# First keys ahead of the last seeds' stores, first maxima by pairs, and copies that lie interleaved, in a kernel of a state-space convolution beside attention

## The chip, the cores and the metric

The kernel runs on one core of one Trainium2 chip. The metric is the time of one execution on the device in microseconds (us); the time of a version is the median of its runs.

## The reference

Two independent operators on sequences of 2048 rows and 448 columns, float32, whose results are put side by side:

```python
def _A_ref(u, log_A_real, A_imag, C_real, C_imag, log_dt, D_skip):
    dt = jnp.exp(log_dt)
    A = -jnp.exp(log_A_real) + 1j * A_imag
    C = (C_real + 1j * C_imag) * dt[:, None]
    P = jnp.exp((A * dt[:, None])[:, :, None] * pos[None, None, :])
    K = 2.0 * jnp.einsum("dn,dnl->dl", C, P).real      # 448 x 2048, from 256 states each
    ...                                                # y = causal convolution of u with K, by FFT
    return y + u * D_skip[None, None, :]

def _B_ref(x, wqkv, wo):                               # 16 heads of 28
    q, k, v = qkv[0], qkv[1], qkv[2]
    scores = jnp.einsum("bhqd,bhkd->bhqk", q, k) * scale
    p = _softmax(scores, axis=-1)
    o = jnp.einsum("bhqk,bhkd->bhqd", p, v)
    return (lambda x, *d: x.transpose(*d))(o, 0, 2, 1, 3).reshape(B, S, D) @ wo

    return jnp.concatenate([a, b], axis=-1)
```

## The kernel before, in words

Everything is written with a tile framework that works out the waits between instructions. All of it lies in one function, `body`; a helper object records every instruction, which is why every row of the profile names line 75 and groups are told apart by the names of their tiles.

**First part.** Its instructions are put in order on each engine by the framework's planner, which goes by the order of the program and its own idea of when operands are ready. Two kinds of work are woven together over 41 stages (`n_stage`, the loop `for t in range(n_stage)`).

- Projections. The input `x` is taken in four chunks of 512 rows (`load_x`, tiles `xn`, transposed into `xh` and `xl`). Forty-eight jobs, twelve a chunk, make keys, queries (`qk_proj`, 12 matmuls each, for one group of four heads) and values (`v_proj`). Every float32 value is held as a high and a low part. `project()` issues the matmuls of the next job and then the evacuation (`evac`) of the one before: ScalarE writes the high part, VectorE the low part, both into a tile `hl` of which there are three, and SyncE stores it to DRAM (`k<-hl`, `q<-hl`). The weights lie in the memory that later holds the keys of the first group (`k0_t`, by the name `khat`), head index for head index, so the keys of head j can only be loaded when the projections of group j are over.
- Seeds. For eight groups `o` of channels, `seeds(o)` lists thirteen steps that make starting values for the powers of the state-space kernel. A group starts four stages after the one before. Two tiles come out: `se` in a buffer of the ring `qhat` (three buffers, shared with the query tiles) and `sg` (two buffers). `put_g` and `put_e`, the last two steps, store them (`sd<-sg`, `sd<-qhat`).

The list `ahead` puts loads for the attention into the stages: key differences (`load_kd`, from stage `A0` on), the first query tile (`load_q(0)`, in two halves at stages `A1` and `A1 + 1`), the keys of heads 0 to 2 (`load_k`, at the stages in `KW`). After the last projection come the keys of head 3, the second query tile, and the values. All of these DMAs are issued by SyncE, in order of the program.

A query or key tile holds, for 28 features and two spare rows of a head, four copies of 32 rows on the 128 partitions: high and low parts combined so that one matmul gives all four products. A copy lies on 32 neighbouring partitions, and each copy is a DMA of its own.

**First maxima.** The softmax subtracts the row maximum. For query block 0, sixteen tiles of 128 queries go against 2048 keys in four steps (`max_mm(0, i, kc)`). Steps 0 and 1 belong together: step 0 multiplies with the difference of two key blocks (`kdif`), ScalarE takes the relu into `rl`, and step 1 multiplies with the second block and lets VectorE add `rl` and reduce in one pass; relu(a - b) + b is the larger of a and b. Steps 2 and 3 are plain reductions (`mx`). Each step takes one of five PSUM tiles (`pt` or `pm`). `max_join` takes the maximum of the three columns, `max_end` transposes it on TensorE and makes a negative high and low part (`mh`), and `max_put` writes these by two DMAs into the spare rows of the query tile (`qhat<-mh`), so that the score matmul subtracts the maximum by itself.

**Second part.** From here on the program's own order is kept on every engine (`KEPT["a"]`). Three seed tiles are loaded (`load_sd`, `sdb<-sd`), the first three tiles of the next query block's maxima (`LEAD`) are made, and then 256 slots follow with score matmuls (`pss`), exponentials (`p`), products with the values (`po`), maxima of the next query block, and the convolution's work in between, by `ORDER` and due times counted in slots. Keys, queries and key differences of later groups are loaded by the same helpers.

Of the kernel before, what the change touches and what calls it, by code (L numbers as in the profile page):

```python
# [18 lines left out]
D = 448  # L19

H = 16
DH = 28
G = 4
HG = H // G
CQ = 512
# [15 lines left out]
PS = 1  # L41
SGB, XB, XL = 2, 5, 4
K0, KP, KD, UP = 0, 3.5, 4, 3
A0, A1, KW = 26, 34, (33, 35, 36)

N1 = 32
N2 = 64
# [43 lines left out]
def body(ctx, tc, a, out):  # L91
# [53 lines left out]
    def load_k(g, j, p):  # L145
        if j == 0:
            t = k0_t if g == 0 else p.tile([128, HG, L], F32R, name="khat")
            kt_g[g] = [t[:, i] for i in range(HG)]
        for r in range(4):
            nc.sync.dma_start(kt_g[g][j][32 * r:32 * r + 32, :].bitcast(F32), k_d[g][r % 2, 32 * j:32 * j + 32, :])  # L150

    v_g = {}

    def load_v(g, c):
        v_g[g, c] = t = v_p.tile([128, NK // NQ, HG, 32], F32, name="v", bufs=5)
        nc.sync.dma_start(t.rearrange("p t h e -> p t (h e)"), v_d[c][:, g])

    def load_kd(g, j, rows=range(4)):
        if 0 in rows:
            kd_g[g, j] = kd_p.tile([128, CQ], F32R, name=f"kdif{j}")  # L160
        t = kd_g[g, j]
        for r in rows:
            nc.sync.dma_start(t[32 * r:32 * r + 32].bitcast(F32), kd_d[g][r % 2, 32 * j:32 * j + 32, :])

    def load_q(u, rows=range(4)):
        g, c = divmod(u, NQ)
        if 0 in rows:
            q_u[u] = q_p.tile([128, HG, CQ], F32R, name="qhat", bufs=3)
        t = q_u[u]
        for r in rows:  # L170
            nc.sync.dma_start(t[32 * r:32 * r + 32].bitcast(F32), q_d[g][c][r // 2].rearrange("(j p) q -> p j q", j=HG))

    def max_mm(u, i, kc, ps=w_tile):

# [16 lines left out]
            nc.tensor.matmul(pm, q, kt[:, kc * CQ:(kc + 1) * CQ], start=True, stop=True)  # L191
            nc.vector.tensor_reduce(mx, pm, axis=AX.X, op=ALU.max)

    def max_join(u):
        m_u[u, 1] = q_p.tile([128, HG * 4], F32, name="m1", bufs=2)
        nc.vector.tensor_reduce(m_u[u, 1], m_u[u].rearrange("p a b c -> p (a b) c"), axis=AX.X, op=ALU.max)

    def max_end(u, ps):
        nc.tensor.transpose(ps[:16, :128], m_u[u, 1], ident)
# [3 lines left out]
                                       op0=ALU.mult, op1=ALU.subtract)  # L203
        mh_u[u] = mh

    def max_put(u):
        for i in range(2):
            nc.sync.dma_start(q_u[u][DH + i:DH + i + 1, :, :].rearrange("p h (t q) -> p (h t) q", t=4).bitcast(F32),
                                mh_u[u][:, i, :].bitcast(F32))


    with ExitStack() as st:
# [12 lines left out]
        def load_x(c):  # L225
            xs = x[c * CQ:(c + 1) * CQ, :].rearrange("(t p) d -> p t d", p=128)
            for h in range(2):
                xns[c, h] = y_p.tile([128, 2, D], F32, name="xn", bufs=3)
                nc.sync.dma_start(xns[c, h], xs[:, 2 * h:2 * h + 2, :])

        load_x(0)
# [24 lines left out]
                                                            ap=[[256, JF // 4], [JF * 256, 4], [1, 256]]))  # L256

        dt_all = s_p.tile([PO, 5, NO], F32, name="dt_all")
        ldt = s_p.tile([NO, PO], F32, name="ldt")
        t = a["A_log_dt"]  # L260
        for f in range(2):
            nc.sync.dma_start(ldt[4 * f:4 * f + 4, :].rearrange("o (j i) -> o j i", j=4), bass.AP(
# [16 lines left out]

        def exact_exp(y, x_, shape):  # L280

            t = lambda n, d=F32: s_p.tile(shape, d, name=n)
            ts, stt = nc.vector.tensor_scalar, nc.vector.scalar_tensor_tensor
            x1, kf, r1, p, ki = t("x1"), t("kf"), t("r1"), t("px"), t("ki", I32)
            ts(x1, x_, -87.0, 88.0, op0=ALU.max, op1=ALU.min)
            ts(kf, x1, 1.4426950408889634, MAGIC, op0=ALU.mult, op1=ALU.add)
            ts(kf, kf, MAGIC, None, op0=ALU.subtract)
            stt(r1, kf, -0.693359375, x1, op0=ALU.mult, op1=ALU.add)
            stt(r1, kf, 2.12194440e-4, r1, op0=ALU.mult, op1=ALU.add)
            ts(p, r1, 1.0 / 5040, 1.0 / 720, op0=ALU.mult, op1=ALU.add)  # L290
            for q in (120.0, 24.0, 6.0, 2.0, 1.0):
                nc.vector.tensor_tensor(p, p, r1, ALU.mult)
                ts(p, p, 1.0 / q, None, op0=ALU.add)
            nc.vector.tensor_tensor(p, p, r1, ALU.mult)
            ts(kf, kf, 127.0, 8388608.0, op0=ALU.add, op1=ALU.mult)
            nc.vector.tensor_copy(ki, kf)
            stt(y, p, 1.0, ki.bitcast(F32), op0=ALU.add, op1=ALU.mult)

        dt8 = s_p.tile([NO, PO], F32, name="dt8")
        exact_exp(dt8, ldt, [NO, PO])  # L300
        dt_o = s_p.tile([NO, PO], F32, name="dt_o")
        nc.vector.tensor_copy(dt_o.rearrange("o (i j) -> o j i", j=4), dt8.rearrange("o (j i) -> o j i", j=4))

        def turn_dt():
# [153 lines left out]
        def qk_proj(c, s, g):  # L458
            pp = w_tile()
            n = 0  # L460
            for k in range(NCK):
                for i, x_ in ((0, xh), (1, xh), (0, xl)):
                    nc.tensor.matmul(pp, w_g[:, i, s, k, g].rearrange("p h e -> p (h e)"), x_[k],
                                     start=n == 0, stop=n == 3 * NCK - 1)
                    n += 1

            def evac():
                hl = x_p.tile([128, 2, CQ], F32R, name="hl", bufs=3)
                th, tl = hl[:, 0], hl[:, 1]
                if s == 1:  # L470
                    nc.scalar.activation(th, pp, AF.Identity, bias=kones)
                    nc.vector.scalar_tensor_tensor(tl, pp, kones, th.bitcast(F32), op0=ALU.add, op1=ALU.subtract)
                else:
                    nc.scalar.activation(th, pp, AF.Copy)
                    nc.vector.tensor_tensor(tl, pp, th.bitcast(F32), ALU.subtract)
                if s == 1 and c < 2:
                    HC = CQ // 2
                    kb = y_p.tile([128, HC], F32, name="kb")
                    dhl = y_p.tile([128, 2, HC], F32R, name="dhl")
                    dh, dl = dhl[:, 0], dhl[:, 1]  # L480
                    nc.scalar.activation(kb, pp[:, HC:], AF.Copy)
# [32 lines left out]
        stages = [seeds(o) for o in range(NO)]  # L514
        n_stage = SP * (NO - 1) + len(stages[0])
        slots = [[] for _ in range(n_stage)]
        for o in range(NO):
            for i, st_ in enumerate(stages[o]):
                slots[max(SP * o + (i or -2), 0)] += st_
# [6 lines left out]
        for i in range(2):  # L526
            ahead[A1 + i].append(lambda i=i: load_q(0, range(2 * i, 2 * i + 2)))

        for j, t in enumerate(KW):
            ahead[t].append(lambda j=j: load_k(0, j, k0_p))  # L530

        def project():

            e = work.pop(0)() if work else None
            while pend:
                pend.pop(0)()
            if e:
                pend.append(e)

        for t in range(n_stage):  # L540
            while work and n_work - len(work) < n_work * (t + 1) / PW:
                project()
            for f in slots[t] + ahead.get(t, []):
                f()
            if t + 1 == PW:
                project()
                wst.close()
                load_k(0, HG - 1, k0_p)
                load_q(1)
                for c in range(NQ):  # L550
                    load_v(0, c)
        xst.close()
        more = [lambda: ps_t.tile([128, CQ], F32, name="pt")] * 2 + [w_tile] * 3
        for i in range(16):
            for kc in range(4):
                max_mm(0, i, kc, more[(4 * i + kc) % 5])
        nc.scalar.activation(half_pi[:1], half_pi[:1], AF.Exp)
        max_join(0)
        max_end(0, ps_t.tile([128, CQ], F32, name="pt"))
        max_put(0)  # L560
        sst.close()


# [59 lines left out]

    sds, egs = {}, {}

    def load_sd(b):
        sds[b] = g_p.tile([128, SDF], F32, name="sdb", bufs=4)
        nc.sync.dma_start(sds[b], sd_d[b // BO][b % BO])

    def k_seeds(b):  # L630

# [241 lines left out]

    nc.kept = KEPT["a"]
    for b in range(3):
        load_sd(b)
    for i in range(LEAD):
        for kc in range(4):
            max_mm(1, i, kc)
# [260 lines left out]
```

## Time and profile before

| | us |
|---|---|
| median of 3 runs | 1284.48 (1284.33 to 1285.08) |
| profiled execution | 1284.77 |
| its span on the core | 1283.0 |
| TensorE busy in the span | 1221.8 |
| last projection matmul starts | 183.22 |
| first matmul of the first maxima starts | 194.86 |
| first score matmul (`pss`) starts | 234.70 |

Times inside the span count from its start. PE is TensorE, PEld its weight loads, DVE VectorE, ACT ScalarE, POOL GpSimd, SP SyncE (SPq its queue, in which each DMA is an issue). A row of the order of time gives the start, the time it took, engine, operation and tiles, and in brackets the idle time of the engine before it with what ended that. A row of the waits gives the total, the count and the longest. A row of a stretch gives its length, then for each engine busy time and instructions, then the clock granted to TensorE as a share, the busy share of the 16 DMA engines, and GB/s. A wait for several semaphores is put down to the one that came last by the profile.

### The profile page before, as it was taken

The numbers are of one execution on the slowest core, as the hardware profiler recorded it, in microseconds if no ns is written. First come the engines' busy times: TensorE is split into PE (matmuls) and PEld (weight loads), VectorE is DVE, ScalarE is ACT, GpSimd is POOL, SyncE is SP. The second block draws the span as 40 slices with busy tenths as digits, with TensorE's granted clock in tenths as the row PEclk, the third lists the DMA queues.
The fourth block names the chain that finished last, engine by engine and source line by source line (L and its number), as shares of the span: only waits on it lengthen the run. The fifth ranks groups of instructions, "written<-read, shape, count | busy, mean of one in ns | idle before, by whom it ended". The sixth has DMA issues, their size and how long they took to land.

```text
span 1283.0 us, 33256 instructions
## 1 busy us (share of the span) xinstructions
PE 1221.8 (95%) x12625; PEld 696.6 (54%) x12625; DVE 931.8 (73%) x2106; ACT 957.1 (75%) x2142; POOL 844.4 (66%) x728
## 2 busy tenths in 40 slices
PE   7988857999999999999999999999999999999997
PEld 5867743555555555555555555555555555544433
DVE  5788878877877787878778988888897645645111
ACT  4979852688888888888888888888887756656552
POOL 2466750698878888887689999989995222324321
PEclk9989888899999999999999999999999999999999
DMA  7867799447764645478643233742325543657666
GB/s 212 264 243 264 247 307 273 127 95 171 182 153 103 153 133 147 133 204 206 169 101 90 63 73 81 163 103 71 82 60 148 166 143 134 204 162 238 200 162 173
DMA packets 200088, 205.36 MB, mean 160 GB/s; under 512 B 95992, under 2 KB 158520, under 8 KB 197880
## 3 DMA queue, kind: packets, MB, share of 16 engines
q1 hardware_dynamic: 199928, 203.23, 57.1%
q8 instruction: 100, 1.64, 0.6%
q14 instruction: 60, 0.49, 0.1%
HBM read 120.73 MB, written 82.18 MB: 158 GB/s over the span
## 4 chain that ended last, share of the span: by engine, by line
PE 75%; DVE 11%; ACT 4%; POOL 4%; issue 3%; DMA 2%; SPq 0%; POOLq 0%; ACTq 0%; DVEq 0%
PE pm L75 42%; PE pss L75 16%; PE po L75 16%; DVE mx L75 2%; POOL e L75 1%; ACT tri L75 1%; DVE sg L75 1%; DVE tri L75 1%; DVE rl L75 1%; DVE px L75 1%; DVE hl L75 1%; DMA khat<-k 1%; DVE qhat L75 1%; POOL p L75 1%; DMA tri<-in_B_wqkv 1%
## 5 line engine op out<-in xcount | busy, mean ns | idle before, releaser
L75 ACT ACTIVATE p<-pss 128x512 f32<-128x512 f32 x1024 | 561.4, 611 | 112.2 <-PE pss L75 106.8
L75 PE MATMUL pss<-qhat,khat 128*128 128x512 f32 x1024 | 403.4, 400 | 1.7 <-ACT p L75 1.7
L75 DVE TENSOR_REDUCE mx<-pm 128x1 f32<-128x512 f32 x500 | 321.7, 684 | 110.2 <-PE pm L75 108.0
L75 PE MATMUL pm<-khat,qhat 128*128 128x512 f32 x749 | 327.2, 440 | 3.2 <-DVE mx L75 2.1
L75 POOL TENSOR_TENSOR e<-e,sdb 128x256 f32<-128x256 f32 x168 | 201.8, 1201 | 118.2 <-ACT e L75 108.9
L75 PE MATMUL po<-p,v 128*32 128x512 f32 x2048 | 269.2, 594 | 0.0
L75 POOL TENSOR_TENSOR e<-e,eu 128x256 f32<-128x256 f32 x168 | 248.2, 1477 | 13.2
L75 PEld LDWEIGHTS pm<-khat,qhat 128*128 128x128 f32 x749 | 141.9, 190 | 199.1 <-ACT p L75 49.5
L75 DVE CUSTOM_DVE_ANT_0 rl<-pm,rl 128x512 f32<-128x512 f32 x249 | 171.5, 689 | 65.5 <-ACT rl L75 62.4
L75 PEld LDWEIGHTS pss<-qhat,khat 128*128 128x128 f32 x1024 | 190.7, 189 | 46.5 <-issue 10.8
L75 POOL TENSOR_TENSOR eu<-e,sdb 128x256 f32<-128x256 f32 x168 | 201.9, 1202 | 0.0
L75 POOL TENSOR_TENSOR p<-pr,pr 64x448 f32<-64x448 f32 x64 | 73.1, 1142 | 159.6 <-PE pm L75 134.2
L75 ACT ACTIVATE rl<-pm 128x512 f32<-128x512 f32 x249 | 151.2, 607 | 20.9 <-PE pm L75 16.4
L75 DVE TENSOR_TENSOR g<-g,zg 128x128 f32<-128x128 f32 x392 | 162.2, 414 | 3.4
L75 PE MATMUL pm<-kdif,qhat 128*128 128x512 f32 x249 | 101.3, 407 | 2.4 <-DVE mx L75 1.3
L75 PE MATMUL pm<-xh,khat 112*128 112x512 f32 x256 | 86.9, 421 | 13.7 <-DVE hl L75 5.2
L75 DVE TENSOR_TENSOR zg<-g,zg 128x128 f32<-128x128 f32 x224 | 87.9, 393 | 5.0
L75 PEld LDWEIGHTS pm<-e,g 128*32 128x32 f32 x3584 | 57.2, 109 | 43.8 <-issue 16.7
L75 DVE TENSOR_TENSOR pr<-pm,ub 128x448 f32<-128x448 f32 x64 | 37.0, 620 | 56.4 <-PE pm L75 42.0
L75 PE MATMUL pm<-e,g 128*32 128x64 f32 x3584 | 73.0, 222 | 1.9 <-POOL e L75 1.9
L75 ACT ACTIVATE y<-pm 128x448 f32<-128x448 f32 x48 | 26.5, 553 | 58.2 <-PE pm L75 34.1
L75 ACT ACTIVATE ub<-pm 128x224 f32<-128x224 f32 (+1 forms) x96 | 38.8, 449 | 39.7 <-PE pm L75 37.4
(134 smaller groups left out, 1445.3 us busy)
## 6 DMA issues: line engine op xcount, KB each, us to landing
sdb<-sd SPq DMA_DIRECT2D x56, 336.0 KB
khat<-k SPq DMA_DIRECT2D x64, 256.0 KB
qhat<-q SPq DMA_DIRECT2D x64, 256.0 KB
sd<-sg SPq DMA_DIRECT2D x8, 1456.0 KB
k<-hl SPq DMA_DIRECT2D x16, 512.0 KB
q<-hl SPq DMA_DIRECT2D x16, 512.0 KB
mw<-in_mw SPq DMA_DIRECT2D x16, 512.0 KB
sd<-qhat SPq DMA_DIRECT2D x8, 896.0 KB
```

What stands on the lines that cost most here:

```text
L75: i = f(*args, **kw)
```

## The change

- The four copies of keys, key differences and queries lie interleaved: copy r takes every fourth partition from r on (`[r::4]`) instead of 32 neighbours. The row of maxima goes to the partitions that follow from it.
- The first query tile is loaded from stage 31 on instead of 34. The keys of the first three heads are loaded by `project()` itself, each behind the evacuation that follows the end of its weights; those of head 3 ahead of the last evacuation.
- The two stores of seed group 6 (`kept_e`, `kept_g`) leave their stages: one goes between the first values and the second query tile, the other behind all values.
- The query evacuations of the last chunk use the three input tiles `xn` (widened from 448 to 512 columns) instead of `hl`.
- Steps 2 and 3 of the first maxima are done as a pair as well (`max_pair`): step 2 accumulates two matmuls, with the query tile and its negative `q_neg`, into the difference, relu on ScalarE, and step 3 adds and reduces. `q_neg` is made by four ScalarE copies. `max_join` then reads two columns.
- The two row DMAs of the first maxima and the load of the first seed tile are issued by ScalarE instead of SyncE.
- The small temporaries of the channel time steps lie in a seed buffer.

```diff
-A0, A1, KW = 26, 34, (33, 35, 36)
+A0, A1 = 26, 31
...
-            nc.sync.dma_start(kt_g[g][j][32 * r:32 * r + 32, :].bitcast(F32), k_d[g][r % 2, 32 * j:32 * j + 32, :])
+            nc.sync.dma_start(kt_g[g][j][r::4, :].bitcast(F32), k_d[g][r % 2, 32 * j:32 * j + 32, :])
...
-            nc.sync.dma_start(t[32 * r:32 * r + 32].bitcast(F32), kd_d[g][r % 2, 32 * j:32 * j + 32, :])
+            nc.sync.dma_start(t[r::4].bitcast(F32), kd_d[g][r % 2, 32 * j:32 * j + 32, :])
...
-            nc.sync.dma_start(t[32 * r:32 * r + 32].bitcast(F32), q_d[g][c][r // 2].rearrange("(j p) q -> p j q", j=HG))
+            nc.sync.dma_start(t[r::4].bitcast(F32), q_d[g][c][r // 2].rearrange("(j p) q -> p j q", j=HG))
+
+    def max_pair(i, kc, ps, q_neg):
+        j, t = divmod(i, 4)
+        ts = slice(t * 128, (t + 1) * 128)
+        pm, kt = ps(), kt_g[0][j]
+        if kc == 2:
+            nc.tensor.matmul(pm, q_u[0][:, j, ts], kt[:, 2 * CQ:3 * CQ], start=True, stop=False)
+            nc.tensor.matmul(pm, q_neg[:, j, ts], kt[:, 3 * CQ:], start=False, stop=True)
+            rl_u[0, i] = kd_p.tile([128, CQ], F32, name="rl", bufs=2)
+            nc.scalar.activation(rl_u[0, i], pm, AF.Relu)
+        else:
+            nc.tensor.matmul(pm, q_u[0][:, j, ts], kt[:, 3 * CQ:], start=True, stop=True)
+            rl = rl_u.pop((0, i))
+            nc.vector.tensor_tensor_reduce(rl, pm, rl, 1.0, -3.0e38, ALU.add, ALU.max, m_u[0][:, j, t, 1:2])
...
-    def max_put(u):
+    def max_put(u, queue=nc.sync):
         for i in range(2):
-            nc.sync.dma_start(q_u[u][DH + i:DH + i + 1, :, :].rearrange("p h (t q) -> p (h t) q", t=4).bitcast(F32),
+            queue.dma_start(q_u[u][4 * (DH + i):4 * (DH + i) + 1, :, :].rearrange("p h (t q) -> p (h t) q", t=4).bitcast(F32),
                                 mh_u[u][:, i, :].bitcast(F32))
...
-                xns[c, h] = y_p.tile([128, 2, D], F32, name="xn", bufs=3)
+                xns[c, h] = y_p.tile([128, 2, CQ], F32, name="xn", bufs=3)[:, :, :D]
...
-                hl = x_p.tile([128, 2, CQ], F32R, name="hl", bufs=3)
+                if c == NQ - 1 and s == 0:
+                    hl = y_p.tile([128, 2, CQ], F32, name="xn", bufs=3).bitcast(F32R)
+                else:
+                    hl = x_p.tile([128, 2, CQ], F32R, name="hl", bufs=3)
...
+        kept_g, kept_e = (stages[NO - 2][i] for i in (-2, -1))
+        stages[NO - 2][-2:] = []
...
-        for j, t in enumerate(KW):
-            ahead[t].append(lambda j=j: load_k(0, j, k0_p))
-
         def project():
 
-            e = work.pop(0)() if work else None
+            j, last = divmod(len(work) - 1, 2)
+            e = work.pop(0)() if work else load_k(0, HG - 1, k0_p)
             while pend:
                 pend.pop(0)()
             if e:
                 pend.append(e)
+            if e and not last and j < HG - 1:
+                load_k(0, HG - 2 - j, k0_p)
...
                 wst.close()
-                load_k(0, HG - 1, k0_p)
+                load_v(0, 0)
+                kept_e.pop()()
                 load_q(1)
-                for c in range(NQ):
+                for c in range(1, NQ):
                     load_v(0, c)
+                kept_g.pop()()
         xst.close()
         more = [lambda: ps_t.tile([128, CQ], F32, name="pt")] * 2 + [w_tile] * 3
+        n_st = ExitStack()
+        q_neg = pool(n_st, "n_p").tile([128, HG, CQ], F32R, name="q_neg")
+        for j in range(HG):
+            nc.scalar.activation(q_neg[:, j], q_u[0][:, j].bitcast(F32), AF.Copy, scale=-1.0)
         for i in range(16):
             for kc in range(4):
-                max_mm(0, i, kc, more[(4 * i + kc) % 5])
+                f, kw = (max_mm, (0, i, kc)) if kc < 2 else (max_pair, (i, kc))
+                f(*kw, more[(4 * i + kc) % 5], *([q_neg] if kc > 1 else []))
         nc.scalar.activation(half_pi[:1], half_pi[:1], AF.Exp)
-        max_join(0)
+        n_st.close()
+        max_join(0, 2)
         max_end(0, ps_t.tile([128, CQ], F32, name="pt"))
-        max_put(0)
+        max_put(0, nc.scalar)
...
-    def load_sd(b):
+    def load_sd(b, queue=nc.sync):
         sds[b] = g_p.tile([128, SDF], F32, name="sdb", bufs=4)
-        nc.sync.dma_start(sds[b], sd_d[b // BO][b % BO])
+        queue.dma_start(sds[b], sd_d[b // BO][b % BO])
...
     for b in range(3):
-        load_sd(b)
+        load_sd(b, nc.sync if b else nc.scalar)
```

More of the change, by code (lines that the diff above doesn't have):

```diff
@@ L192, in max_mm, with max_join @@
             nc.vector.tensor_reduce(mx, pm, axis=AX.X, op=ALU.max)
-    def max_join(u):
+    def max_join(u, n=3):
         m_u[u, 1] = q_p.tile([128, HG * 4], F32, name="m1", bufs=2)
-        nc.vector.tensor_reduce(m_u[u, 1], m_u[u].rearrange("p a b c -> p (a b) c"), axis=AX.X, op=ALU.max)
+        nc.vector.tensor_reduce(m_u[u, 1], m_u[u].rearrange("p a b c -> p (a b) c")[:, :, :n], axis=AX.X, op=ALU.max)
     def max_end(u, ps):
@@ L258, in body @@
         dt_all = s_p.tile([PO, 5, NO], F32, name="dt_all")
-        ldt = s_p.tile([NO, PO], F32, name="ldt")
+        small = s_p.tile([128, BO, SDF - F_G], F32, name="sg", bufs=SGB)
+        small = iter([small[:NO, i, :PO] for i in range(BO)] + [small[:NO, i, PO:2 * PO] for i in range(BO)])
+        ldt = next(small)
         t = a["A_log_dt"]
@@ L280, in exact_exp @@
         def exact_exp(y, x_, shape):
-            t = lambda n, d=F32: s_p.tile(shape, d, name=n)
+            t = lambda n, d=F32: next(small) if d == F32 else next(small).bitcast(d)
             ts, stt = nc.vector.tensor_scalar, nc.vector.scalar_tensor_tensor
@@ L297, in exact_exp @@
             stt(y, p, 1.0, ki.bitcast(F32), op0=ALU.add, op1=ALU.mult)
-        dt8 = s_p.tile([NO, PO], F32, name="dt8")
+        dt8 = next(small)
         exact_exp(dt8, ldt, [NO, PO])
-        dt_o = s_p.tile([NO, PO], F32, name="dt_o")
+        dt_o = next(small)
         nc.vector.tensor_copy(dt_o.rearrange("o (i j) -> o j i", j=4), dt8.rearrange("o (j i) -> o j i", j=4))
```

## The prediction

> **What bounds the kernel now.** I read the page first, then the stretches of time, then the waits and the queue of SyncE around the one place where TensorE stands still.
>
> ```profile
> span 1283.0 us, 33256 instructions
> PE 1221.8 (95%) x12625; PEld 696.6 (54%) x12625; DVE 931.8 (73%) x2106; ACT 957.1 (75%) x2142; POOL 844.4 (66%) x728
> ```
>
> The profiled execution took 1284.77 us, 1.8 around its span and 0.3 over the median of the three timed runs (1284.48), so what I work out on the trace is taken off the median as it stands. TensorE fills the span, but not evenly. Busy time in four stretches (PE, PEld, DVE, ACT, POOL, granted clock, DMA share, GB/s):
>
> ```profile
> 184.00:194.80 10.80, 0.00 (x0) 0.00 (x0) 3.87 (x8) 1.73 (x5) 3.64 (x4) 0.58 1.08 314
> 194.86:226.70 31.84, 25.75 (x64) 12.44 (x64) 29.18 (x64) 9.55 (x16) 0.00 (x0) 0.93 1.04 281
> 226.70:234.70 8.00, 7.61 (x15) 3.98 (x15) 5.91 (x16) 2.29 (x5) 1.08 (x2) 0.50 0.63 191
> 234.70:1283.00 1048.30, 1031.84 (x11843) 555.29 (x11841) 748.18 (x1738) 801.55 (x1771) 734.46 (x577) 1.00 0.52 138
> ```
>
> From 234.7 on TensorE is busy 1031.84 of 1048.30 us, in an order written out by hand that the change leaves alone; there only copies of keys and queries arrive in another layout, beside DMA engines that are half idle. So that stretch keeps its length, and what counts is when its first score matmul starts. Ahead of it are an idle hole of 11 us, the first maxima (64 matmuls in 31.84 us, VectorE busy 29.18 of them), and 8 us for maxima of the next query block. The DMA engines are full (share over 1) through hole and maxima. What holds the hole open (waits, then the queue of SyncE):
>
> ```profile
> PE pt L75 <- DMA khat<-k: 11.2, 1, 11.2
> ACT hl L75 <- DMA k<-hl: 5.5, 1, 5.5
> 176.14 1.98 SPq L75 DMA_DIRECT2D khat<-k  x4
> ...
> 181.68 0.50 SPq L75 DMA_DIRECT2D sd<-sg  x1
> 182.22 1.60 SPq L75 DMA_DIRECT2D qhat<-q  x2
> 183.92 3.40 SPq L75 DMA_DIRECT2D khat<-k  x4
> 188.15 0.38 SPq L75 DMA_DIRECT2D k<-hl  x1
> 192.21 0.38 SPq L75 DMA_DIRECT2D sd<-qhat  x1
> 193.34 0.32 SPq L75 DMA_DIRECT2D khat<-k  x1
> 194.53 0.32 SPq L75 DMA_DIRECT2D khat<-k  x1
> SPq L75 <- DMA sd<-sg: 3.6, 1, 3.6
> ```
>
> SyncE itself waits for landings: counting DMAs, each issue here goes out when the one eight before it has landed. The store of 192.21 stands eight after `sd<-sg` of 181.68; the khat load of 194.53 stands eight after the second qhat load of the pair at 182.22. So that store landed about 192.2, and the last quarter of the query tile at 194.5, 0.3 us ahead of the first maximum (194.86, in the rows further down). The first four tiles use only the keys of 176.14; I read the wait, put down to khat, as one for the query tile, which stood behind a seed store.
>
> **The change part by part.** Rates first: DMAs per kind (KB each), then two stretches in which only 32-row loads land and two with the v loads and with a seed store; the last two figures are DMA share and GB/s.
>
> ```profile
> khat<-k SPq DMA_DIRECT2D x16, 256.0 KB
> sd<-sg SPq DMA_DIRECT2D x3, 1456.0 KB
> sd<-qhat SPq DMA_DIRECT2D x3, 896.0 KB
> q<-hl SPq DMA_DIRECT2D x4, 512.0 KB
> 209.00:215.00 6.00, 5.45 (x15) 2.36 (x15) 6.00 (x14) 1.79 (x3) 0.00 (x0) 1.00 1.02 209
> 215.00:220.00 5.00, 3.33 (x10) 1.55 (x9) 4.07 (x9) 1.79 (x3) 0.00 (x0) 1.00 1.05 210
> 220.40:222.70 2.30, 2.01 (x6) 0.84 (x6) 2.30 (x6) 0.60 (x1) 0.00 (x0) 1.00 1.05 393
> 222.70:226.60 3.90, 1.95 (x5) 0.69 (x5) 3.90 (x9) 0.60 (x1) 0.00 (x0) 1.00 1.04 367
> ```
>
> *Copies interleaved.* A load of one copy writes 32 neighbouring partitions: 256 KB at 209 GB/s, 1.25 us. The v loads write as many bytes to 128 partitions at 393 GB/s, 0.67 us. Keys come in 8 KB runs and queries in 2 KB runs at the same 209 and 210, so the partitions matter, not the run. After the change a copy's 32 rows are every fourth partition of all 128. No row shows that; the ends are 0.67 and 1.25, and nothing here suggests dearer. I take 0.75, nearer the v row. The Trainium skill, page "SBUF — State Buffer", section "Door 1: The DMA port swizzle", says the same: partitions 0 to 31 reach 8 of 16 ports (189 GB/s there), all 128 reach 16 (328); the two rates here agree in kind, and its ratio would make an estimate of 0.72, by which the sum below stays what it is.
>
> *Keys ahead of seed stores, queries earlier.* The query tile goes three stages up, and the stores of the seventh seed group (1456 KB at 367 GB/s, 4.1 us; 896 KB, 2.5 us) go behind all keys. In the queue at 170 then follow, ahead of the first maximum: four query quarters (4 x 0.75), first keys (4 x 0.75), and what was there already. The first keys were all in before SyncE could issue its next load at 183.92; queries add 3.0 ahead of them, faster keys give back 2.0, one q store of 1.3 falls behind them. So first keys and queries are there at about 183.9 + 3.0 - 2.0 - 1.3, say 183.5 (187 at 1.25, where queries add 5.0 and keys give nothing back). Behind come five `hl` stores (512 KB at about 390 GB/s, 1.3 each, 6.5), 12 key quarters (9.0), one v load (0.7), the `sd<-qhat` store (2.5) whose buffer the second query tile takes and for which SyncE must therefore stand (between the 0.3 of an issue and the 3.6 of its wait for a seed store; I take 2), and four quarters of that tile (3.0): 183.5 + 6.5 + 9 + 0.7 + 2.5 + 2 + 3 = 207. A head's keys arrive every 4 to 5 us and serve 5.6 us of maxima (below). The remaining stores (4.1 + 4.1 + 2.5) and v loads end about 220; they delay nobody, as their data are read late.
>
> *Last q in the input's tiles.* ScalarE's 5.5 us wait for an `hl` buffer goes. What is late next is TensorE's own end, and then VectorE's seed work:
>
> ```profile
> 183.22 0.39 PE L75 MATMUL pm<-xl,khat 112*128 112x512 f32 x1
> 185.38 0.69 DVE L75 TENSOR_TENSOR hl<-pm,hl 128x512 fp32r<-128x512 f32 x1 [2.78 <-ACT hl L75]
> 188.81 0.55 DVE L75 TENSOR_TENSOR sg<-sg,px 128x224 f32<-128x224 f32 x1
> 194.86 0.76 PE L75 MATMUL pt<-kdif,qhat 128*128 128x512 f32 x1 [11.25 <-DMA khat<-k]
> 200.06 0.39 PE L75 MATMUL pt<-khat,qhat 128*128 128x512 f32 x1
> 200.29 0.40 PE L75 MATMUL pm<-kdif,qhat 128*128 128x512 f32 x1
> ```
>
> Projections end at 183.6; evacuation by ScalarE 0.6 and VectorE 0.69 to 184.9; then the seed work, which before runs from that row's end (186.0) to 189.4, 3.4 us: to 188.3. In that time ScalarE negates the query tile: four copies of 512 columns, no row here, at 0.6 each by the 0.597 of `rl` below 2.4 us, under the seed work unless the planner puts it later (then up to 2.4 on the path). I let VectorE's part of the maxima begin at 188.3 instead of 196.29.
>
> *First maxima by pairs.* Groups of the stretch 194.8 to 226.7:
>
> ```profile
> L75 DVE CUSTOM_DVE_ANT_0 rl<-pm,rl 128x512 f32<-128x512 f32 x9 | 6.1, 682 | 1.2 <-PE pm L75 1.2
> L75 ACT ACTIVATE rl<-pm 128x512 f32<-128x512 f32 x9 | 5.4, 597 | 11.9 <-PE pm L75 11.9
> 205.81 0.60 DVE rl L75
> 208.21 1.21 DVE mx L75 x3
> ```
>
> Per tile VectorE now does one `rl` and two `mx` passes, 0.60 + 1.21 = 1.81 by the chain, and 16 x 1.81 = 29. It will do two `rl` passes, 1.22; ScalarE two relus, 1.2; TensorE five matmuls instead of four, 5 x 0.23 = 1.2 at full clock. All three are equal, so latency decides: a PSUM tile that waits for the relu is held for a matmul, a relu and a pass less one matmul's pitch, 0.45 + 0.60 + 0.69 - 0.23 and three hand-overs of 0.05, 1.66 us; five tiles serve four uses per step, 1.66 x 4/5 = 1.33. I take 1.4, ends 1.22 and 1.81. 16 x 1.4 = 22.4, and 0.6 for a first tile at the half clock that an idle stretch leaves (0.58 granted in the hole; five matmuls then take 2.3): the maxima end at 188.3 + 23.0 = 211.3 instead of 226.7.
>
> *Row and first seeds on ScalarE's queue.* Rows of the hand-over:
>
> ```profile
> 227.80 1.27 SPq L75 DMA_DIRECT2D qhat<-mh  x2
> 228.12 0.60 ACT L75 ACTIVATE rl<-pm 128x512 f32<-128x512 f32 x1 [4.46 <-DVE mh L75]
> 234.70 0.63 PE L75 MATMUL pss<-qhat,khat 128*128 128x512 f32 x1
> ```
>
> SyncE no longer stands until the row is ready. ScalarE now issues two row DMAs (1.27) and a seed load (about 0.6) and has the relus of the next block's maxima queued behind; at 0.3 to 0.6 each that is 0.9 to 1.9, and TensorE, with three PSUM tiles, waits for those relus. I take 1.5 on the path. The row's own flight stays under the 12 maxima.
>
> Temporaries in a seed buffer and wider input tiles cost nothing: same instructions, at a time when nothing waits for them.
>
> *Sum.* Hand-over as before (234.7 - 226.7 = 8.0) plus 1.5: the first score matmul at 211.3 + 9.5 = 220.8 instead of 234.7, the second query tile (207) being there. 13.9 us less: 1284.5 - 13.9 = 1270.6.
>
> **Rivals.** *A, scattered rows load no faster (1.25).* For: 16 engines are full already, in time if not in bytes. Against: the v row. First keys at 187; then 6.5 + 15 + 0.7 + 2.5 + 2 + 5 puts the second query tile at 218.7, the maxima of the next block wait for it and take 8: first score 227, 7.7 less, 1277.
>
> *B, the pairs hang on ScalarE or the clock.* With 1.81 per tile as now, the maxima end at 188.3 + 29 + 0.6 = 218, first score at 227.4: 7.3 less, 1277. Against: ScalarE is busy 9.55 of 31.84.
>
> *C, slower: ScalarE stands on landings.* Its queue is in order, and rows load at 1.25; if its seed load's memory or counter hangs on the last seed stores, the relus and soon the exponentials stand behind it. At 0.75 the stores end at 220, and the relu to the first score is 6.6 (228.12 to 234.70): 227, still 7 less. At 1.25 they end 12 later, at 232, first score at 239: 4.5 more, 1289. It turns the sign once ScalarE is released later than 228.1. The Trainium skill, "DMA: Bandwidth & Descriptors", section "Issuing engines are not separate DMA queues", holds that DMAs of another engine's queue share the same 16 engines, so the row would meet the stores there too; no run here shows a DMA from ScalarE.
>
> *D, no gain:* the planner of the first part orders it so that the maxima start no sooner, and B holds too: about 1284.
>
> **How the numbers follow.** The forecast has 0.69 (its own range 1265 to 1274), A 0.13, B 0.07, C 0.07, D 0.04. Below the forecast lie hand-over matmuls at full clock (12 at 1.81 per four is 5.4, 2 less) and ScalarE issues at 0.9. So 1264 to 1279 takes in A and B. Within 0.2% (2.6 us, about what a measurement of this kernel can tell from no change): D, 0.04. Slower: C, and 0.01 of the forecast for what no row shows, 0.08; faster, the rest of it with A and B, 0.88.
>
> **What would show it.** Right: no hole over 5 us after the last projection; `rl` passes alone on VectorE at a pitch near 0.7 in some 23 us; loads of keys at over 300 GB/s; first `pss` near 221, the rest 1048 us. Wrong: SyncE or ScalarE idle on landings in front of `qhat` or `sdb`, key loads still at 209 GB/s, a stretch behind the first `pss` that is longer.

## The result, and the profile after

The changed kernel takes 1282.18 us, median of 20 runs (1279.76 to 1284.67), against 1284.47 for the kernel before on the same chip: 0.998 of its time, interval 0.9974 to 0.9987. The forecast was 1270.6 in a range of 1264 to 1279. Of the 13.9 us it expected, 2.3 came.

The head of the page after, then five stretches cut where those of before were cut: hole, maxima at the half clock, maxima at the full clock, hand-over, the rest.

```profile
span 1282.8 us, 33335 instructions
PE 1223.7 (95%) x12641; PEld 700.9 (55%) x12641; DVE 925.5 (72%) x2106; ACT 967.8 (75%) x2162; POOL 843.4 (66%) x728
```

```profile
182.00:195.00 13.00, 2.44 (x5) 1.22 (x5) 10.71 (x23) 3.08 (x11) 11.85 (x18) 0.55 1.01 357
195.00:203.50 8.50, 7.18 (x15) 4.58 (x16) 4.32 (x13) 6.52 (x13) 1.74 (x2) 0.50 1.02 390
203.50:225.00 21.50, 17.83 (x61) 9.94 (x60) 17.23 (x53) 14.30 (x25) 0.00 (x0) 1.00 0.65 231
225.00:234.40 9.40, 7.10 (x14) 3.64 (x15) 5.79 (x15) 2.30 (x5) 1.08 (x2) 0.64 0.66 210
234.40:1282.80 1048.40, 1031.03 (x11843) 554.38 (x11841) 748.14 (x1738) 801.11 (x1771) 734.32 (x577) 1.00 0.47 139
```

The last row is the stretch that the forecast kept: 1048.4 after, 1048.3 before. The hole is still there, but the busy engines in it are now VectorE (10.71 of 13) and GpSimd (11.85 of 13). The DMA engines are no longer full after 203.5 (0.65; before over 1). TensorE's rows show what the hole is made of:

```profile
179.81 0.40 PE L75 MATMUL pm<-xl,khat 112*128 112x512 f32 x1
181.90 0.47 PE L75 MATMUL pt<-kdif,qhat 128*128 128x512 f32 x1 [1.70 <-issue]
188.93 0.79 PE L75 MATMUL pm<-kdif,qhat 128*128 128x512 f32 x1 [6.56 <-DVE xn L75]
...
196.06 1.53 PE L75 MATMUL pt<-khat,qhat 128*128 128x512 f32 x2 [5.05 <-ACT rl L75]
...
234.41 0.41 PE L75 MATMUL pss<-qhat,khat 128*128 128x512 f32 x1
```

The last projection matmul starts 3.4 us sooner than before (183.22), and the first step of the first maximum runs at 181.90, 13 us sooner than before: query tile and key difference are there. Then TensorE fills its PSUM tiles and stands, in the end for `rl`, ScalarE's relu of that first step. ScalarE's order says why the relu comes at 195.37:

```profile
186.88 0.39 ACT L75 ACTIVATE gz<-gz 128x224 f32<-128x224 f32 x1 [1.92 <-POOL gz L75]
...
187.52 0.63 ACT L75 ACTIVATE xn<-pm 128x512 fp32r<-128x512 f32 x1
192.93 0.58 ACT L75 ACTIVATE sg<-pn 128x112 f32<-128x112 f32 x2 [4.78 <-DVE px L75]
195.01 0.57 ACT L75 ACTIVATE sg<-px 128x112 f32<-128x112 f32 x2 [1.50 <-DVE sg L75]
195.37 0.63 ACT L75 ACTIVATE rl<-pt 128x512 f32<-128x512 f32 x1
195.90 2.17 ACT L75 ACTIVATE q_neg<-qhat 128x512 fp32r<-128x512 f32 x4
```

The relu stands in order behind the last seed group's copies (`sg`), which wait for VectorE's products, and those for `gz`, which comes from GpSimd. GpSimd before, and then after (the fill of the seventh seed group's buffer, and `gz` of the eighth):

```profile
141.20 0.51 POOL L75 MEMSET qhat<- 128x112 f32 x2
...
171.45 0.67 POOL L75 TENSOR_TENSOR gz<-tri 128x224 f32<-128x224 f32 x1 [1.51 <-DVE px L75]
```

```profile
161.81 0.56 POOL L75 MEMSET qhat<- 128x112 f32 x2
...
176.80 1.29 POOL L75 TENSOR_TENSOR tri<-tri 128x224 f32<-128x224 f32 x1 [11.97 <-ACT tri L75]
...
186.20 0.65 POOL L75 TENSOR_TENSOR gz<-tri 128x224 f32<-128x224 f32 x1
```

The fill is 20.6 us later, and `gz` of the eighth group 14.75 (some 2 us of each are an earlier loss, below). The reason lies in one line of the change. Query tiles and the seeds' `se` tiles share a ring of three buffers, handed out in the order of the program. The seventh group's (`o` = 6) `se` is asked for at stage 32. Before, the query tile came behind it (stage 34); at stage 31 it comes ahead and takes the buffer that was free at 141; this is called the claim below. The group then has to wait for the next buffer, until an older group has been stored (issued at 151.32). That is ten us ahead of the fill: the rest is the planner's order, which now has the fill behind the group's own product of 160.87. And since its work is now late, the planner sets it behind a product of the eighth group (`tri`, 176.80) that waits 11.97 for ScalarE's sines.

The one profiled execution took 1284.67, the longest of the 20. It is about 2 us late well ahead of the change: in the stretch from 95 to 110 the clock granted to TensorE was 1.00 before and 0.77 here.

```profile
95.00:110.00 15.00, 12.00 (x59) 8.85 (x58) 11.95 (x23) 14.14 (x38) 9.26 (x13) 1.00 0.76 243
```

```profile
95.00:110.00 15.00, 12.39 (x52) 9.63 (x50) 10.07 (x18) 13.74 (x35) 8.54 (x12) 0.77 0.72 231
```

Some profiles of the variants below show such a dip there and some don't. So lengths are compared inside one execution, and versions by their medians.

### The profile page after: what moved, and what is told of

Its sections match the earlier page's. It is cut to its first block, busy times and chain, and to the rows that moved or that the text cites. A ratio compares the mean times of both kernels' runs of the same rounds, so it can differ in the third digit from the quotient of the medians.

```text
span 1282.8 us, 33335 instructions
## 1 busy us (share of the span) xinstructions
PE 1223.7 (95%) x12641; PEld 700.9 (55%) x12641; DVE 925.5 (72%) x2106; ACT 967.8 (75%) x2162; POOL 843.4 (66%) x728
## 4 chain that ended last, share of the span: by engine, by line
PE 77%; DVE 7%; ACT 5%; POOL 5%; issue 3%; DMA 2%; SPq 0%; ACTq 0%; POOLq 0%; DVEq 0%
PE pm L75 44%; PE pss L75 16%; PE po L75 16%; POOL e L75 1%; ACT tri L75 1%; DVE mx L75 1%; ACT rl L75 1%; PE pt L75 1%; POOL qhat L75 1%; DVE sg L75 1%; DVE hl L75 1%; DVE tri L75 1%; POOL x_e L75 1%; DVE px L75 1%; POOL p L75 1%
## 5 line engine op out<-in xcount | busy, mean ns | idle before, releaser
L75 DVE TENSOR_REDUCE mx<-pm 128x1 f32<-128x512 f32 x480 | 308.6, 684 | 109.6 <-PE pm L75 107.5
L75 DVE CUSTOM_DVE_ANT_0 rl<-pm,rl 128x512 f32<-128x512 f32 x259 | 178.4, 689 | 71.6 <-ACT rl L75 68.4
L75 ACT ACTIVATE rl<-pm 128x512 f32<-128x512 f32 x259 | 157.1, 607 | 12.7 <-PE pm L75 7.9
```

The source lines that it names most:

```text
L75: i = f(*args, **kw)
```

## The experiments

Theory 1, from the rows above: the claim of the ring's buffer, through the order that the planner then chooses, holds the first relu at 195, and hides what every other part does. Rival: one of the parts (interleaving, pairs, ScalarE's DMAs) does not work.

**e1, the query tile one stage later.**

```diff
-A0, A1 = 26, 31
+A0, A1 = 26, 32
```

> The changed kernel with the first query tile loaded from stage 32 on instead of 31, behind the step of seed group 6 that takes a buffer of the same ring of three. Theory 1 (the early load takes the free buffer of the ring, seed group 6 waits for the next one, its products on GpSimd come 16 us later than before, group 7 queues behind them, and ScalarE, in order, reaches the first relu only at 195.4): the memset of group 6 is back near 141 instead of 161.8, the first relu comes at 187 to 190, the first score matmul at 226 to 229 instead of 234.6, the time falls by 5 to 8 us, to about 1275. Rival 2 (the loop of the maxima itself is what ate the gain, by its negated copies, a half clock and latency): first relu moves, but the loop stretches as much, 1281 to 1283. Rival 3 (key loads bound the start): first relu stays at 195, waiting for khat.

Measured: 1275.76 (1272.2 to 1278.13), 0.993 of before (0.9918 to 0.9942). GpSimd, ScalarE and TensorE:

```profile
140.74 0.51 POOL L75 MEMSET qhat<- 128x112 f32 x2
171.57 0.67 POOL L75 TENSOR_TENSOR gz<-tri 128x224 f32<-128x224 f32 x1 [2.11 <-DVE px L75]
```

```profile
185.88 0.58 ACT L75 ACTIVATE sg<-px 128x112 f32<-128x112 f32 x2 [1.51 <-DVE sg L75]
186.24 0.65 ACT L75 ACTIVATE rl<-pt 128x512 f32<-128x512 f32 x1
```

```profile
185.25 0.76 PE L75 MATMUL pt<-kdif,qhat 128*128 128x512 f32 x1 [6.82 <-DMA qhat<-q]
...
223.57 0.40 PE L75 MATMUL pss<-qhat,khat 128*128 128x512 f32 x1
```

The fill is back at 140.74, `gz` at 171.57, the first relu comes 9.1 us sooner than in the changed kernel (about 2 of it the dip above), and 6.4 us come off the median by a load that is issued *later*. Relu and first score (223.57) come a little sooner than expected. What holds the start now is the query tile's last quarter and, 0.4 us ahead of the relu, again the seeds' copies.

**e12, the claim alone.** It takes the stage out of the question. The load stays at stage 32, and only the order inside that stage is turned, so that the query tile asks for its buffer ahead of the seeds.

```diff
-            for f in slots[t] + ahead.get(t, []):
+            early = ahead.pop(t, []) if t == A1 else []
+            for f in early + slots[t] + ahead.get(t, []):
```

> As the run with the query tile at stage 32 (1275.8), but within that stage the loads are written ahead of the stage's seed steps instead of behind them, so that the query tile takes the free buffer of the ring before the seventh seed group does; the stage, and with it the loads' place among the key and seed DMAs, stays. Theory 1 (the order of the claim): GpSimd's fill of the seventh group goes from 141 to 160 or later, the last query evacuation stands behind the seeds again, first score at 229 or later, 1281 to 1284. Rival (it was the stage, with two more loads in SyncE's queue one stage sooner): 1275 to 1277.

Measured: 1282.07 (1281.1 to 1285.69), 0.9981 (0.9972 to 0.999): the whole gain of e1 is gone, and theory 1 is shown. GpSimd, then ScalarE:

```profile
175.72 0.80 POOL L75 TENSOR_TENSOR tri<-tri 128x224 f32<-128x224 f32 x1 [14.61 <-ACT tri L75]
176.46 0.56 POOL L75 MEMSET qhat<- 128x112 f32 x2
```

```profile
179.47 0.57 ACT L75 ACTIVATE xn<-pm 128x512 fp32r<-128x512 f32 x1
...
187.61 0.39 ACT L75 ACTIVATE gz<-gz 128x224 f32<-128x224 f32 x1 [3.66 <-POOL gz L75]
...
195.56 0.57 ACT L75 ACTIVATE sg<-px 128x112 f32<-128x112 f32 x2 [1.50 <-DVE sg L75]
195.93 0.64 ACT L75 ACTIVATE rl<-pt 128x512 f32<-128x512 f32 x1
```

The fill comes even later than in the changed kernel, behind the product of the eighth group. The turned order also puts the first query quarters ahead of one seed store in SyncE's queue, and the first step runs at 188.98 instead of e1's 185.25; but the relu comes some 6 us after that step's end, so it is the order on ScalarE that holds it, and not a load. One detail of the expectation was wrong: the last query evacuation (`xn`) does not stand behind the seeds here (179.47; 187.52 in the changed kernel), and the time is the same. So the 6.56 that TensorE waited for `xn` in the changed kernel cost nothing; the chain over `gz` sets the start by itself.

**e2, e3, e4: the parts, with the claim in place.** Each undoes one part of the changed kernel. e2 puts all copies back on 32 neighbours, e3 makes steps 2 and 3 of the first maxima plain again, e4 gives row and first seed back to SyncE.

```diff
-            nc.sync.dma_start(kt_g[g][j][r::4, :].bitcast(F32), k_d[g][r % 2, 32 * j:32 * j + 32, :])
+            nc.sync.dma_start(kt_g[g][j][32 * r:32 * r + 32, :].bitcast(F32), k_d[g][r % 2, 32 * j:32 * j + 32, :])
...
-                f, kw = (max_mm, (0, i, kc)) if kc < 2 else (max_pair, (i, kc))
-                f(*kw, more[(4 * i + kc) % 5], *([q_neg] if kc > 1 else []))
+                max_mm(0, i, kc, more[(4 * i + kc) % 5])
...
-        max_put(0, nc.scalar)
+        max_put(0)
...
-        load_sd(b, nc.sync if b else nc.scalar)
+        load_sd(b)
```

> The changed kernel with every copy again on 32 neighbouring partitions (keys, key differences, queries, and the row of maxima). Theory 1: loads take 1.2 us a quarter instead of 0.62, the first keys come about 191 instead of 186.6, still ahead of ScalarE's first relu at 195.4; later heads and the second query tile come up to 10 us later, so the time rises by 0 to 5 us. Rival 3 (key loads bound the start): the first relu moves by as much as the keys, 5 us or more, and the time rises by 8 or more.

> The changed kernel with steps 2 and 3 of the first maxima as plain reductions again, without the negated query tile. Theory 1 with a loop that loses most of its gain: the maxima start where they do now, without 2.2 us of negated copies on ScalarE, and run 16 x 1.81 = 29 us, so that they end within 1 us of where they end now: 1281 to 1284. If the pairs gain the 6 us that were forecast: 1287 or more. If they are a loss by the half clock: 1279 to 1280.

> The changed kernel with the row of the first maxima and the first seed tile issued by SyncE again. The changed trace has 1.9 us of issues on ScalarE (225.9 to 227.8) ahead of the relu that TensorE waits for. If that is on the path: the relu comes 1.5 to 2 us sooner and the time falls by 1 to 2 us. If the hand-over hides it (maxima of the next block paced by the half clock): no change within 0.5 us.

| | median (range) | ratio to before | interval |
|---|---|---|---|
| changed kernel | 1282.18 (1279.76 to 1284.67) | 0.998 | 0.9974 to 0.9987 |
| e2, 32 neighbours | 1281.52 (1280.36 to 1282.43) | 0.9975 | 0.9967 to 0.9984 |
| e3, no pairs | 1282.47 (1280.6 to 1283.55) | 0.9981 | 0.9973 to 0.999 |
| e4, row on SyncE | 1279.25 (1278.13 to 1284.77) | 0.9969 | 0.9958 to 0.9981 |

Under the claim neither interleaving nor pairs can be told from nothing. Without ScalarE's DMAs (e4) the median is 2.9 lower, but the intervals overlap, and three of the twelve runs of e4 took 1283.66 or more; the traces under e7 say more.

**e5, e6, e7: the same parts, without the claim** (each with the query tile at stage 32, as in e1; the edits are those of e2, e3, e4).

> Query tile at stage 32 as in the run before it that had this alone (1275.8, first maximum released by the query tile's last quarter at 185.1), copies written on 32 neighbouring partitions again. Theory 1 (the claim of the seeds' buffer hid every other part): now the loads set the start, so slower ones show. Query quarters and first keys at 1.2 instead of 0.62 each, eight of them ahead of the first maximum: 8 x 0.6 = 4.8 later; time 1279 to 1282. Rival (rate of these loads never matters): 1275 to 1277.

> Query tile at stage 32, the plain four maxima per tile, no negated copy. Theory 1: in the changed kernel the pairs gained nothing because the negated copy (2.2) and the half clock took what the shorter step gave; with a full clock from 188 a tile costs 1.81 instead of about 1.45, 16 x 0.36 = 5.8, less the 2.2 of the copy: 3.6 slower than with pairs, 1279 to 1280. Rival (pairs are worth nothing at any clock): 1275 to 1277.

> Query tile at stage 32, and the maxima's row and the first seed load on SyncE's queue again. If ScalarE's three issues cost what they cost with the query tile at stage 31 (3 us from 1282.2 to 1279.25), 1273. Rival: SyncE, which stores and loads on landings until about 200, is itself late with the row now that the maxima end 10 us sooner: 1276 to 1280, with the relu waiting on a SyncE issue that comes later than 216.

| | median (range) | ratio to before | interval |
|---|---|---|---|
| e1 | 1275.76 (1272.2 to 1278.13) | 0.993 | 0.9918 to 0.9942 |
| e5, 32 neighbours | 1278.76 (1278.09 to 1281.04) | 0.9956 | 0.9943 to 0.9968 |
| e6, no pairs | 1276.56 (1276.51 to 1278.26) | 0.9937 | 0.9924 to 0.9951 |
| e7, row on SyncE | 1272.45 (1271.85 to 1274.74) | 0.9907 | 0.9894 to 0.9921 |

e5 is 3.0 slower than e1 (4.8 was the size of the term; 1279 to 1282 was expected, and the median is just under it): now the loads set the start, and TensorE's first matmul waits for the query tile until 189.66 instead of 185.25.

```profile
189.66 0.77 PE L75 MATMUL pt<-kdif,qhat 128*128 128x512 f32 x1 [9.59 <-DMA qhat<-q]
```

e6 is where theory and median part. Inside the profiled executions the pairs do what was said of them. At the full clock a plain tile takes 1.81 (first fence, VectorE in e6: 201.27 to 203.08), a tile in pairs 1.43 at best (second fence, e1: 200.32 to 201.75), and 1.53 in the mean of e1's 13 ordinary tiles, without the first, the twelfth and the last. VectorE's part of the maxima takes 27.4 in e1 and 30.9 in e6.

```profile
201.27 0.68 DVE L75 CUSTOM_DVE_ANT_0 rl<-pm,rl 128x512 f32<-128x512 f32 x1
203.08 0.68 DVE L75 CUSTOM_DVE_ANT_0 rl<-pm,rl 128x512 f32<-128x512 f32 x1
```

```profile
200.32 0.69 DVE L75 CUSTOM_DVE_ANT_0 rl<-pt,rl 128x512 f32<-128x512 f32 x1
...
201.75 0.69 DVE L75 CUSTOM_DVE_ANT_0 rl<-pt,rl 128x512 f32<-128x512 f32 x1
```

Yet the medians of e1 and e6 differ by 0.8, not by the 3.6 expected, and their intervals overlap. The profiled execution of e1 was the fastest of its five and that of e6 the slowest of its five. What the pairs are worth in time stays open.

e7 is 3.3 below e1, close to the 1273 expected, and 9.7 below the changed kernel: the lowest median here. Against e1 the intervals overlap a little, and the two profiled executions took the same (1272.34 and 1272.2), so the medians alone do not show the 3.3. The traces show the part of it that lies in the hand-over. That of e7 (SyncE, ScalarE, TensorE), and then that of the changed kernel:

```profile
215.59 2.04 SPq L75 DMA_DIRECT2D qhat<-mh  x2
...
215.69 0.60 ACT L75 ACTIVATE rl<-pm 128x512 f32<-128x512 f32 x1 [1.84 <-PE pm L75]
...
222.26 0.58 PE L75 MATMUL pss<-qhat,khat 128*128 128x512 f32 x1
```

```profile
225.91 1.25 ACTq L75 DMA_DIRECT2D qhat<-mh  x2
227.19 0.59 ACTq L75 DMA_DIRECT2D sdb<-sd  x1
227.83 0.60 ACT L75 ACTIVATE rl<-pm 128x512 f32<-128x512 f32 x1 [3.69 <-DMA qhat<-mh]
```

With the row on SyncE the relu of the next maxima runs while the row is being issued; on ScalarE it stands behind three issues, 1.9 us. From VectorE's last step of the first maxima (`m<-mx`) to the first score matmul it is 9.2 to 9.5 in all seven traces with the row on ScalarE (changed kernel, e1, e2, e3, e5, e6, e12), and 7.7 in all five with pairs and the row on SyncE (e4, e7 to e10).

**e8, e9, e10: beyond e7.** e8 writes each head's negated copy just ahead of that head's tiles, e9 loads all four query quarters at stage 32, e10 adds the copies on GpSimd to e9; all three have the row on SyncE, as e7.

```diff
-        for j in range(HG):
-            nc.scalar.activation(q_neg[:, j], q_u[0][:, j].bitcast(F32), AF.Copy, scale=-1.0)
         for i in range(16):
+            if i % 4 == 0:
+                nc.scalar.activation(q_neg[:, i // 4], q_u[0][:, i // 4].bitcast(F32), AF.Copy, scale=-1.0)
...
-            ahead[A1 + i].append(lambda i=i: load_q(0, range(2 * i, 2 * i + 2)))
+            ahead[A1].append(lambda i=i: load_q(0, range(2 * i, 2 * i + 2)))
...
-            nc.scalar.activation(q_neg[:, j], q_u[0][:, j].bitcast(F32), AF.Copy, scale=-1.0)
+            nc.gpsimd.tensor_scalar(q_neg[:, j], q_u[0][:, j].bitcast(F32), -1.0, None, op0=ALU.mult)
```

> The run before this one in the list, and each head's negated copy just ahead of that head's first tile instead of all four ahead of the first tile. Theory: three of the four copies (0.54 each) leave the path in front of the first steps and go under VectorE's passes: 1.6 less, 1271 to 1272. Rival: VectorE's passes hang on ScalarE's relus at the pitch of 1.45, so a copy costs its 0.54 wherever it stands: same as the run before.

> As the run with the query tile at stage 32 and the row on SyncE (1272.45, first maximum at 185.6 to 186.6 behind the last query quarter), but all four query quarters at stage 32 instead of two there and two a stage later. Theory: the last query quarter was the only thing late, and lands some 7 us sooner; then the first keys (two quarters of 0.62 behind them, about 184) or VectorE's seed work release the first maximum, at 183.5 to 185: 1 to 2 us less, 1271. Rival: the same bytes stand ahead of the first maximum in either order, so nothing moves: 1272.5.

> The run before it, with the negated copies on GpSimd, which is idle there. Theory: 2.18 of ScalarE's time leaves the front of the pairs; GpSimd's first copy must be done before the third step of the first tile (about 1 us after its relu): 1 to 2 less than the run before, 1269 to 1270. Rival: GpSimd is so slow at it (over 3 us for one copy of 512 columns) that the third step waits for it: the same or 1 to 2 more.

None gains. e8: 1273.2 (ratio 0.9913, 0.9901 to 0.9926); the planner put three of the four copies in front all the same (first row below), so it tells nothing of its theory. e9: 1274.2 (0.9916, 0.9902 to 0.9929), in kind its rival: the first step runs at 181.29, but the next waits for keys, which now land behind the queries (second and third row), and the clock is granted in half until 193.2, where in e7 it is full from 190 on. e10: 1274.72 (0.9918, 0.9905 to 0.9931): GpSimd was expected to be idle, but its seed work runs to 191.4, and the copies take 1.46 each behind it (last row).

```profile
187.91 1.66 ACT L75 ACTIVATE q_neg<-qhat 128x512 fp32r<-128x512 f32 x3
```

```profile
181.29 0.47 PE L75 MATMUL pt<-kdif,qhat 128*128 128x512 f32 x1 [1.70 <-DMA qhat<-q]
185.26 0.77 PE L75 MATMUL pt<-khat,qhat 128*128 128x512 f32 x1 [3.28 <-DMA khat<-k]
```

```profile
191.40 5.86 POOL L75 TENSOR_SCALAR q_neg<-qhat 128x512 fp32r<-128x512 f32 x4
```

**e11, the kernel before with its query tile at stage 32.**

```diff
-A0, A1, KW = 26, 34, (33, 35, 36)
+A0, A1, KW = 26, 32, (33, 35, 36)
```

> The kernel before with one number changed: its query tile at stage 32 instead of 34. Theory (what the changed kernel can gain comes mostly from the query tile standing ahead of the seed store, as the hole of 11 us in front of the first maximum was its wait): the first maximum comes at 188 to 190 instead of 194.9, behind VectorE's seed work, and 1278 to 1280 follows. Rival (that hole is a wait for the full DMA engines, whatever their order): 1284 to 1285.

Measured: 1282.71 (1281.45 to 1285.49), 0.9984 (0.9975 to 0.9993): 1.8 us, not the 4.5 to 6.5 expected. TensorE, then the stretch of VectorE's part of the maxima:

```profile
189.18 0.76 PE L75 MATMUL pt<-khat,qhat 128*128 128x512 f32 x1 [3.56 <-DMA khat<-k]
```

```profile
190.10:225.70 35.60, 27.80 (x62) 15.90 (x60) 30.24 (x65) 9.55 (x16) 0.00 (x0) 0.64 1.05 293
```

The first step no longer waits for the query tile (it runs at 185.15), but the next ones wait for keys, which come at the old rate and behind the seed stores, and ScalarE waits for `hl` again (3.04). VectorE's part begins 6.2 sooner than before, at 190.10, but lasts 5.2 longer: TensorE waits for keys inside it (1.5 and 1.8), and the granted clock over it is 0.64, where it was 0.93 before. Neither theory had that. So the earlier query tile alone gains little; which of the missing parts holds it back is not separated here. Keys at the old rate alone do not: e5 has them, and is 6 us below before.

## Why the prediction failed

By its own sum, with the version that has no claim and no ScalarE DMAs beside it (all inside one profiled execution):

| step | forecast | changed kernel | e7 |
|---|---|---|---|
| VectorE's part of the maxima begins | 188.3 | 196.04 | 187.20 |
| to its end | 23.0 | 28.8 | 27.4 |
| hand-over to the first score | 9.5 | 9.5 | 7.7 |
| first score | 220.8 | 234.4 | 222.3 |
| from there to the end | 1048.3 | 1048.4 | 1048.3 |

The starts and ends are VectorE's first and last `rl` passes (changed kernel, then e7):

```profile
196.04 0.69 DVE L75 CUSTOM_DVE_ANT_0 rl<-pt,rl 128x512 f32<-128x512 f32 x1 [1.06 <-ACT rl L75]
...
224.18 0.69 DVE L75 CUSTOM_DVE_ANT_0 rl<-pm,rl 128x512 f32<-128x512 f32 x1 [0.34 <-ACT rl L75]
```

```profile
187.20 0.69 DVE L75 CUSTOM_DVE_ANT_0 rl<-pt,rl 128x512 f32<-128x512 f32 x1 [1.08 <-ACT rl L75]
...
213.88 0.69 DVE L75 CUSTOM_DVE_ANT_0 rl<-pm,rl 128x512 f32<-128x512 f32 x1 [0.35 <-ACT rl L75]
```

- **The start, 188.3: wrong by 7.7, and the step that failed.** "Keys ahead of seed stores, queries earlier" priced the move of the query tile by SyncE's queue and the DMA rate alone. The tile also takes a buffer, out of a ring that the seeds use, and moving it from stage 34 to 31 moved it past the seventh group's request at stage 32. That is a queue it was moved past, and its price was left out. The working even used the ring, for the second query tile. Without the claim the forecast's start holds within 1.1 us (187.20), and what is late there is in part what was named, VectorE's last seed work with ScalarE's copies behind it; the query tile's last quarter, which the forecast had at 183.5, is as late (e7's first step runs at 185.59).
- **The loop, 23.0: wrong by 5.8.** The pitch of 1.4 is that of the best tiles (1.42 to 1.43); 13 ordinary tiles of e7 take 1.53 in the mean. The negated copies were not hidden: 2.17 of them stand on ScalarE right behind the first relu and ahead of the second. The forecast had named that (up to 2.4 on the path) and left it out of the sum. Next, "0.6 for a first tile at the half clock" was one tile; the clock was granted in half until 203.5, some four tiles. And the twelfth tile takes 2.6 to 2.7 in every version with pairs. It is not explained here, but the kernel before has it too (2.82 instead of 1.81, with TensorE idle for 1.30), so that the sum of 16 equal tiles left it out. In e7 the clock is full from 190 on, and the loop still takes 27.4 instead of 22.4 (16 tiles of 1.4): there the copies cost 1.7, the twelfth tile 1.2, and the 13 ordinary tiles 0.13 each, 1.7.

```profile
190.00:214.60 24.60, 20.84 (x71) 11.66 (x70) 20.40 (x62) 16.88 (x30) 0.00 (x0) 1.00 0.96 341
```

- **The hand-over, 9.5: right** in total. The three issues on ScalarE were taken at 1.5; without them it is 7.7 in e7, so 1.8 in the trace; by the medians 2.9 and 3.3 (e4, e7), with intervals that overlap.
- **Interleaved copies, 0.75 a load: right and a little cautious.** Between 195 and 203.5 (the second stretch of the profile after), where mostly keys land, DMA moved 390 GB/s, 0.67 for 256 KB, where 209 was shown before. By the Trainium skill, "SBUF — State Buffer", section "Door 1: The DMA port swizzle", the estimate was 0.72; the trace's 0.67 agrees nearly.
- **The stretch behind the first score: right**, 1048.4; in the variants between 1046.4 (e3) and 1050.8 (e5).
- **The rivals.** A did not come: the rows load at 390 GB/s. B's price came (28.8, where it had 29 and 0.6), by ScalarE's copies, the half clock and the twelfth tile. D, the planner orders the first part so that the maxima start no sooner, and B holds too, is nearly what came, and it had 0.04. It was written as a possibility without a mechanism; looking for one would have led to the ring. C did not come: SyncE did stand on ScalarE's row for 17.9 us, as the waits of the changed kernel say, but nothing that it had to issue was needed sooner.

```profile
SPq L75 <- DMA qhat<-mh: 17.9, 1, 17.9
```

## What to carry to other kernels

Moving a load earlier also moves its claim on a buffer: before pricing such a move by its queue, list who else asks for that ring's buffers between the old and the new place, and what stands in order behind them on every engine. When a change of several parts moves the time little, look for the one wait that hides them all; here one number (31 to 32) gave 6.4 us and made the faster loads visible. A DMA issued on a compute engine takes its issue time (here 0.6) out of that engine's queue, so put it where nothing is late behind it.

## What the runs showed of the hardware

- Three DMA issues on ScalarE held its next instruction back by 1.9 us, with about 0.6 for each. The Trainium skill, "DMA: Bandwidth & Descriptors", section "Issuing engines are not separate DMA queues", has it that issuing on several engines only saves the sequencer's time to start a DMA, which is usually small relative to the DMA itself. Here the issue time stood on the path: the hand-over is 1.6 to 1.9 us longer in the traces with it.
- A hole in TensorE's work cost twice here, but not by a fixed amount. In the changed kernel the half clock lasted until 203.5, though matmuls had run nearly without a gap since 196.06; in e7, with a shorter hole, matmuls were back at their full-clock time at 188.64, 3 us after the first one (185.59). The length of the hole is not the whole of it: in e9 no idle time ahead of the maxima is over 3.3 us, and the granted clock was 0.50 from 185.26 to 193.2.
- Near 98 to 105 us some executions show a dip of the granted clock that others of the same first part don't (0.77 against 1.00 in the two rows above), and are about 2 us later from there on. One profile is therefore no measure of 2 us.
